# Placing every second head pair on the other partition half in a fused attention and feed-forward kernel

## The chip, the cores and the metric

One Trainium2 chip, one of its cores. The metric is the device time of one execution in microseconds (us), as the median of several runs. The kernel before took 403.56 us (median of 4 runs, 403.14 to 403.96).

The engines are named as the profile names them. PE is the matrix engine, and PEld its weight loads; DVE is the vector engine, ACT the scalar engine with the activation functions, POOL the general engine (GpSimd), SP an engine that here only issues transfers. Each engine works through its own queue in order. PSUM is the memory that PE writes its sums to; DVE and ACT read it and write SBUF, the working memory. Copying a result from PSUM to SBUF is called evicting it. Both memories have 128 partitions, and an engine's cost goes by the elements along a partition.

## What is computed

From the reference, shortened:

```
# q, k, v: (8 batches, 12 heads, 448 positions, 64)
scores = q @ k.T / sqrt(64) - log(448)
attn   = sigmoid(scores) @ v
x      = heads of attn side by side             # 3584 x 768
out    = (silu(x @ w_gate) * (x @ w_val)) @ w_out   # 768 -> 1536 -> 768
```

There is no softmax: each score goes through a sigmoid by itself.

## The kernel before

**Units of attention.** A batch's 12 heads are taken four at a time, which gives 24 units, n = 0 to 23, three to a batch. The four heads of a unit are numbered 2·h2 + w: h2 is the head pair, w the head within the pair. Seven chunks c of 64 key positions make the 448.

**Scores** (`qk_tile`, matmuls at L244). A chunk of a unit is four matmuls of 64 by 64 with 448 columns. The query and key tiles hold pair h2 on partitions 64·h2 onward, so h2 picks the row half of the array; w picks the column half, and with it the PSUM partitions. Bank h2 of a two-bank PSUM tile takes pair h2. One sigmoid on ACT (`sig_tile`, L263; two single-bank ones at L260 at one place in a visit) moves the tile to SBUF as `pt`: head w lies on partitions 64·w onward, for both pairs.

**Attention times values** (`pv`, matmuls at L277). V is loaded with head w on partitions 64·w (`load_v`, L188, one transfer that POOL issues and that turns float32 into float16 on the way). Four matmuls per chunk, one per quadrant of the array. Pair 0 goes to the PSUM half of its own w, pair 1 to the opposite half, since only so all four quadrants are used at once. The next stage wants head w of each pair on partitions 64·w. So pair 0 is evicted by one copy of 128 partitions (L292), and pair 1 by two copies of 64 partitions that cross over (L297 on DVE). Three modes (`how`): 0, all three copies on DVE; 1, one of the crossed copies on ACT after the visit's sigmoids (L305); 2, both on ACT (L300), used once for n = 2.

**Feed-forward, first part.** `ffn1(b, f)` (matmuls at L318) multiplies the six tiles xT[(b, 0..5)] of batch b with one of 12 slices f of w_gate into bank 0 of a PSUM tile and of w_val into bank 1. `ffn1_gate` follows: a sigmoid of bank 0 on ACT (L338), times bank 0 on DVE (L340), times bank 1 on DVE (L344). For f = 0 the order is: tiles 0 to 3 of bank 0, tiles 0 to 3 of bank 1, tiles 4 and 5 of bank 0, tiles 4 and 5 of bank 1, because tiles 4 and 5 come last from attention. For the two last pairs of batches (`LAST - 1` and `LAST`, FAST), eight and twelve slices are instead made by `double`, which does two slices and two batches with seven products (L436) for eight. It needs sums of weights (`fast_w`, DVE, L388), sums of x (`x_sums`, POOL, L409 to L412), evictions by ACT (`snap`, L446) and DVE (L459, L472, L476), and the other activation table (SILU, loaded at L943).

**Feed-forward, second part.** `ffn2_group` (L609) also uses seven products, with sums of h made on DVE (`make_sums`, L530; `budget` says how many after each ffn1) and sums of the remainder on POOL (`rest_sums`, L569). Its evictions go to ACT (L620) for the steps that the string `by` names, else to DVE (L622, L627). The step names are the product numbers 1, 6, 5, 4.

**Order of the work.** PE's order is written out. Up to the ramp's end (about 30 us) it is listed by hand. From there the units of feed-forward work are listed with estimated costs, and "visits" of attention (two to four chunks: two score tiles, then a due `pv`, then the rest of the score tiles, then the sigmoids) are put in between at due times. All PSUM work goes through one ring of four two-bank tiles (`Banked`); a tile can be written again when the readers of its last user are through. A `double` or an ffn1 with f = 0 makes the `pv` that it needs directly ahead of it.

**Transfers.** q and k come through SP (units 4 to 6 through POOL). They are transposed on PE (L214) for the first six units and by transfers that SP issues (L202) from unit 6 on. V and the weights come through POOL's queue. Each transfer that POOL issues takes one of eight semaphores in turn, so POOL may issue a transfer only when the eighth before it has landed.

Of the kernel before, what the change touches and what calls it, by code (L numbers as in the profile page):

```python
# [20 lines left out]
def kernel(  # L21
# [22 lines left out]
    LAST = B // 2 - 1  # L44
# [133 lines left out]
    def load(n, which, eng=None):  # L178
# [4 lines left out]
        (eng or nc.sync).dma_start(out=st, in_=src_of(n, which))  # L183
        qkv_st[(n, which)] = st

    def load_v(n):
        t = v16p.tile([128, 2, S], FP16, tag="v16", name=f"v16_{n}")
        nc.gpsimd.dma_start(out=t, in_=src_of(n, 2))  # L188
        v16[n] = t

    def cast(n, which, eng):
# [43 lines left out]
    xT = {}  # L235

    def qk_tile(n, c, at=None):
        sd = Banked(at=at)
        sc = sd.t
        qt, kt = qT[(n, 0)], qT[(n, 1, c)]  # L240
        for w in range(2):
            for h2 in range(2):
                r = slice(h2 * 64, h2 * 64 + 64)
                nc.tensor.matmul(  # L244
                    out=sc[w * 64:(w + 1) * 64, h2, :S],
                    lhsT=kt[r, w * 64:(w + 1) * 64],
                    rhs=qt[r, :, w * 64:(w + 1) * 64],
                    start=True,
                    stop=True,
                )  # L250
        return sd
# [14 lines left out]
    def pv(n, how=0, at=None):  # L266

        b, j = divmod(n, NJ)
        P = Banked(at=at).t
        vt = v16.pop(n)  # L270
        for c in range(C):
            pt = pts.pop((n, c))
            for h2 in range(2):
                for w in range(2):
                    r = slice(w * 64, w * 64 + 64)
                    g = (w ^ h2) * 64
                    nc.tensor.matmul(  # L277
                        out=P[g:g + 64, h2, :S],
                        lhsT=vt[r, h2, c * D:(c + 1) * D],
                        rhs=pt[r, h2, :],  # L280
                        start=(c == 0),
                        stop=(c == C - 1),
                    )

        def x_tile(h2):
            if n >= NQ - NJ:
                at = 4 * W2 + (2 * j + h2) * S
                return half_of(stg_a)[:, at:at + S]
            return xtp.tile([128, S], FP16, tag="xT", name=f"xT_{b}_{2 * j + h2}")

        x = x_tile(0)
        first = nc.vector.tensor_copy(out=x, in_=P[:, 0, :S])  # L292
        xT[(b, 2 * j)] = x
        x = x_tile(1)
        xT[(b, 2 * j + 1)] = x
        halves = [(x[w * 64:(w + 1) * 64, :], P[(1 - w) * 64:(2 - w) * 64, 1, :S]) for w in range(2)]
        done = [nc.vector.tensor_copy(out=o, in_=i) for o, i in halves[how:]]  # L297
        if how == 2:
            for o, i in halves:
                apart(nc.scalar.copy(out=o, in_=i), first)  # L300

        def rest():
            if how == 1:
                o, i = halves[0]
                apart(nc.scalar.copy(out=o, in_=i), first, *done)  # L305

        return rest


    V, G = nc.vector, nc.gpsimd  # L310
    hT = {}
# [12 lines left out]

    def ffn1(b, f):
        D = Banked("f", made=(b // 2, f))
        for prs in (range(NP - 2), range(NP - 2, NP)) if f == 0 else (range(NP),):
            ffn1_mm(D, b, f, prs)
        ffn1_gate(D, b, f)
        if b % 2:  # L330
            h_sums(b // 2, f)
            make_sums(budget[(b, f)])
        for fn in fill.pop((b, f), ()):
            fn()
# [165 lines left out]
    budget = {}  # L500
# [184 lines left out]
    for pb in range(B // 2):  # L685
# [20 lines left out]
        if pb == 0:  # L706
            fill[(1, 7)] = [lambda: w_sum(0, 3), lambda: w_sum(0, 2)]
            fill[(1, 9)] = [lambda: w_sum(0, 1)]
            o_units += [(0.0, w_sum, a) for a in ((1, 3), (1, 2))]
            part((0, 1, 0, 1), ("1654", "154"), (skip, skip, w((1, 1))))  # L710
            part((0,) * 5, "", (w((0, 4), (1, 4)),))
            copies = [lambda f=f: keep_rest(1, (f, f + 1, f + 2), V.tensor_copy) for f in range(0, NF, 3)]
            part((1,) * 5, "", copies)
            part((2,) * 7, "654")
        elif pb == 1:
            part((0, 1, 0, 1), "1")
            part((0,) * 5)
            part((1,) * 5, "", (lambda: list(rest_sums(1, G)),))
            for g, by in ((2, "54"), (3, "")):
                part((g,) * 3, by)  # L720
                part((g,) * 4, by)
        else:
            part((0, 1) * 7, "1", (skip, lambda: keep_rest(LAST, range(NF), nc.scalar.copy)) if pb < LAST else ())
            if pb == LAST:
                part((3,) * 7)
            part((2,) * 7)
# [22 lines left out]
    def attn_step(group, pvs, how):  # L749
        late = 1 if pvs else 0  # L750
        for part in (group[:2], group[2:]):
            scs = [(n, c, qk_tile(n, c)) for n, c in part]
            rest = [pv(pvs.pop(0), how) for _ in range(len(pvs))]
# [3 lines left out]
            for f in rest:  # L757
                f()

    NPE = 2 * NJ  # L760

# [173 lines left out]
    for i, (fn, args, _) in enumerate(seq):  # L935
        if fn is ffn1:
            ahead = [len(a) if f is None else 0 for f, a, _ in seq[i + 1:i + 3]] + [0, 0]
            budget[args] = 3 if ahead[0] else 0 if ahead[1] == 4 else 2
        if fn is double:
            args[2].append(lambda: make_sums(5))  # L940

# [2 lines left out]
    for fn, args, how in seq:  # L944
        if fn is None:
            pvs, pend = pend, []
            attn_step(args, pvs, how)
# [64 lines left out]
```

## Time and profile before

| | us |
|---|---|
| median of 4 runs | 403.56 |
| the profiled execution, whole time | 403.14 |
| its span (first to last instruction in the profile) | 401.4 |
| outside the span | 1.7 |
| PE busy | 389.2 |
| DVE busy | 262.8 |
| ACT busy | 238.0 |
| POOL busy | 115.1 |
| PE busy from 30 to 397 us | 364.85 of 367 |
| PE busy from 0 to 30 us | 24.35 of 30 |
| mean granted PE clock | 1.00 of full speed |

How to read the rows. A group's row gives line, engine, operation, output and inputs, shape and count, then the busy time and the mean of one in ns, then the engine's idle time ahead of them and what ended it. A row of the timeline gives start, duration, engine, line, operation, count, and in brackets the idle time just before with its releaser. Several instructions of one line are merged into one row, with the count at its end. Ends of matmuls are modelled, so the distance between starts says more about PE than the durations do.

### The profile page before, as it was taken

The page shows a single profiled execution, that of the slowest core. Times are in us where ns is not written, and L with a number is a line of the kernel's source. Part 1 is how long each engine was busy: PE and PEld are TensorE (multiplying, and loading weights), DVE is VectorE, ACT ScalarE, POOL GpSimd, SP SyncE. Part 2 cuts the span into 40 slices and gives each one's busy share as a digit, 9 for nine tenths or more (in the row PEclk, how much of TensorE's full clock was granted, in tenths as well). Part 3 has the DMA queues.
Part 4 walks back from the last instruction along what each step waited for, and adds up shares of the span by engine and source line. Part 5 has one row for each costly group of instructions (what it writes and reads, how often), then busy time and mean ns, then how long its engine had stood idle before and what let it go on. Part 6 is the DMA issues. An engine that isn't in the chain of part 4 may idle for free.

```text
span 401.4 us, 8098 instructions
## 1 busy us (share of the span) xinstructions
PE 389.2 (97%) x3116; PEld 202.4 (50%) x3116; DVE 262.8 (65%) x510; ACT 238.0 (59%) x386; POOL 115.1 (29%) x185
## 2 busy tenths in 40 slices
PE   7799999999999999999999999999999999999995
PEld 3444544445554444444455554444555655555663
DVE  3737657888644555577764457699986568877553
ACT  5965885747457777777753667776654055756000
POOL 4528042311220222222214923910006500000900
PEclk9999999999999999999999999999999999999999
DMA  8999989994599798789785898400000520000055
GB/s 279 243 248 254 246 177 276 167 201 48 136 278 236 161 153 170 162 160 150 174 161 106 227 236 162 47 2 1 2 0 2 157 78 2 2 2 0 2 165 149
DMA packets 65286, 54.39 MB, mean 136 GB/s; under 512 B 35744, under 2 KB 61440, under 8 KB 65248
## 3 DMA queue, kind: packets, MB, share of 16 engines
q1 hardware_dynamic: 49744, 38.22, 37.3%
q0 software_dynamic: 15072, 15.34, 25.0%
q8 instruction: 24, 0.39, 0.5%
q10 hardware_dynamic: 432, 0.33, 0.3%
q14 instruction: 14, 0.11, 0.1%
HBM read 47.19 MB, written 11.01 MB: 145 GB/s over the span
## 4 chain that ended last, share of the span: by engine, by line
PE 91%; DVE 3%; DMA 3%; ACT 1%; issue 1%; SPq 0%; POOL 0%; ACTq 0%; DVEq 0%
PE ps_D L318 32%; PE ps_D L609 24%; PE ps_D L436 20%; PE ps_D L277 8%; PE ps_D L244 8%; DMA v<-in_v_dram 2%; DMA st<-in_q_dram 1%; DVE S L530 1%; DVE xT L297 1%; DVE t L340 0%; PE ps_D L214 0%; ACT pt_a L263 0%; ACT s L338 0%; DVE stg_a L297 0%; DVE xT L292 0%
## 5 line engine op out<-in xcount | busy, mean ns | idle before, releaser
L263 ACT ACTIVATE pt_a<-ps_D 128x896 f16<-128x896 f32 x148 | 127.1, 920 | 42.7 <-PE ps_D L244 41.3
L318 PE MATMUL ps_D<-xT,wg 128*128 128x448 f16 x336 | 74.2, 353 | 0.6 <-DVE t L340 0.5
L318 PE MATMUL ps_D<-xT,wv 128*128 128x448 f16 x336 | 73.7, 352 | 0.0
L340 DVE TENSOR_TENSOR t<-ps_D,s 128x448 f16<-128x448 f32 x56 | 34.9, 624 | 40.4 <-ACT s L338 39.2
L318 PEld LDWEIGHTS <-wg 128*128 128x128 f16 x336 | 30.2, 98 | 36.7 <-issue 12.5
L318 PEld LDWEIGHTS <-wv 128*128 128x128 f16 x336 | 32.8, 98 | 30.8 <-issue 0.4
L446 ACT ACTIVATE snap<-ps_D 128x448 f32<-128x448 f32 x60 | 31.1, 542 | 27.2 <-PE ps_D L436 26.8
L244 PE MATMUL ps_D<-T,T 64*64 64x448 bf16 x644 | 44.4, 357 | 2.7 <-DVE T L220 1.2
L338 ACT ACTIVATE s<-ps_D 128x448 f16<-128x448 f32 x56 | 30.8, 550 | 24.9 <-PE ps_D L318 24.9
L609 PEld LDWEIGHTS <-S 128*128 128x128 f16 x312 | 30.2, 98 | 21.7 <-issue 2.1
L195 POOL CAST c<-stg_a 128x896 bf16<-128x896 f32 x40 | 36.5, 938 | 14.7 <-DMA stg_a<-in_q_dram 10.7
L609 PE MATMUL ps_D<-ramp_a,S 128*128 128x384 f16 x234 | 40.2, 326 | 0.0
L344 DVE SCALAR_TENSOR_TENSOR hT<-ps_D,t 128x448 f16<-128x448 f32 x56 | 35.0, 625 | 5.8
L627 DVE SCALAR_TENSOR_TENSOR osb<-ps_D,osb 128x384 f32<-128x384 f32 x42 | 23.4, 557 | 22.4 <-PE ps_D L609 16.7
L277 PE MATMUL ps_D<-pt_a,v 64*64 64x448 f16 x672 | 36.0, 350 | 0.5 <-DMA v<-in_v_dram 0.5
L622 DVE TENSOR_SCALAR osb<-ps_D 128x384 f32<-128x384 f32 x37 | 20.6, 557 | 18.4 <-PE ps_D L609 15.7
L820 POOL CAST held<-S 128x1 bf16<-128x1 f16 x3 | 0.6, 188 | 107.3 <-ACT osb L620 55.7
L820 POOL CAST held<-pt_a 128x1 bf16<-128x1 f16 x13 | 2.4, 185 | 100.3 <-ACT pt_a L263 100.3
L609 PEld LDWEIGHTS <-hT 128*128 128x128 f16 x228 | 22.0, 98 | 15.8 <-issue 1.3
L292 DVE CAST xT<-ps_D 128x448 f16<-128x448 f32 x21 | 13.1, 624 | 24.0 <-PE ps_D L277 20.9
L244 PEld LDWEIGHTS <-T 64*64 64x64 bf16 x644 | 15.2, 105 | 25.3 <-issue 18.4
L277 PEld LDWEIGHTS <-v 64*64 64x64 f16 x672 | 19.5, 107 | 13.4 <-issue 1.1
(109 smaller groups left out, 503.6 us busy)
## 6 DMA issues: line engine op xcount, KB each, us to landing
out_dram<-osb SPq DMA_DIRECT2D x52, 192.0 KB, 3.2
stg_a<-in_q_dram SPq DMA_DIRECT2D x18, 448.0 KB, 5.7
stg_a<-in_k_dram SPq DMA_DIRECT2D x18, 448.0 KB, 6.4
v<-in_v_dram POOLq DMA_DIRECT2D x24, 224.0 KB, 5.8
wg<-in_moe_w_gate_dram POOLq DMA_DIRECT2D x4, 576.0 KB, 11.9
wv<-in_moe_w_val_dram POOLq DMA_DIRECT2D x4, 576.0 KB, 13.2
wo<-in_moe_w_out_dram POOLq DMA_DIRECT2D x4, 576.0 KB, 8.2
stg_a<-in_q_dram POOLq DMA_DIRECT2D x3, 448.0 KB, 13.8
```

Source lines behind the costliest of these rows:

```text
L195: eng.tensor_copy(out=t.rearrange("p c h d -> p h c d"), in_=st.rearrange("p h (c d) -> p h c d", c=C))
L244: nc.tensor.matmul(out=sc[w * 64:(w + 1) * 64, h2, :S], lhsT=kt[r, w * 64:(w + 1) * 64], rhs=qt[r, :, w * 64:(w + 1) * 64], start=True, st ...
L263: nc.scalar.activation(out=pt, in_=sc[:, :, :S], func=SIGM, bias=sbias, scale=qkscale)
L277: nc.tensor.matmul(out=P[g:g + 64, h2, :S], lhsT=vt[r, h2, c * D:(c + 1) * D], rhs=pt[r, h2, :], start=(c == 0), stop=(c == C - 1),)
L318: nc.tensor.matmul(out=D.t[:, i, :S], lhsT=(wg16, wv16)[i][f // FW][:, pr, cs], rhs=xT[(b, pr)], start=(pr == 0), stop=(pr == NP - 1),),
L338: D.read(nc.scalar.activation(out=s16, in_=D.t[:, 0, :S], func=SIGM), 0)
L340: D.read(nc.vector.tensor_tensor(out=t1, in0=D.t[:, 0, :S], in1=s16, op=MULT), 0)
L344: nc.vector.scalar_tensor_tensor(out=hT[(b // 2, f)][:, b % 2, :], in0=D.t[:, 1, :S], scalar=hsc(b // 2), in1=t1, op0=MULT, op1=MULT),
L436: nc.tensor.matmul(out=D.t[:, bank, :S], lhsT=W(f, j), rhs=X(j), start=(start and j == 0), stop=(stop and j == JT - 1), skip_group_check=True,
L446: D.read(nc.scalar.mul(out=o, in_=D.t[:, bank, :S], mul=scale), bank)
L609: nc.tensor.matmul(out=D.t[:, bank, :hw], lhsT=l, rhs=B_(i), start=(first and i == order[0]), stop=(i == order[-1]), skip_group_check=True,),
L627: D.read(nc.vector.scalar_tensor_tensor(out=o, in0=i, scalar=1.0 / hsc(pb), in1=o, op0=MULT, op1=ADD), bank)
```

## The change

Five edits.

1. For all units but n = 0 (`flip`): the scores of pair 1 go to the opposite PSUM half; V's rows are loaded to match, by two transfers of 64 partitions instead of one of 128 (heads 0 and 3 to the first half, heads 1 and 2 to the second); in `pv` pair 1 uses the opposite row half and its own column half. Both pairs are then evicted by one copy of 128 partitions each: both on DVE, except for n = 2, where the second is on ACT. n = 0 keeps the three copies. The mode that left a copy to ACT behind the sigmoids is gone.
2. ffn1 with f = 0: tiles 0 to 3 of bank 0, 0 to 2 of bank 1, 4 and 5 of bank 0, 3 to 5 of bank 1.
3. In `ffn2_group` for the second pair of batches, group 2: the evictions of steps 5 and 4 go from ACT to DVE.
4. `budget` is 0 for ffn1 (5, 9), so the three sums that were made there are made later.
5. The SILU table is loaded ahead of the `pv` that precedes the first `double`, not behind it.

```
+    def flip(n):
+        return n > 0
+
     def load_v(n):
         t = v16p.tile([128, 2, S], FP16, tag="v16", name=f"v16_{n}")
-        nc.gpsimd.dma_start(out=t, in_=src_of(n, 2))
+        if flip(n):
+            b, j = divmod(n, NJ)
+            src = v[b, 4 * j:4 * j + 4].rearrange("h (p c) d -> p h (c d)", c=C)
+            for w, heads in enumerate((slice(0, 4, 3), slice(1, 3))):
+                nc.gpsimd.dma_start(out=t[w * 64:(w + 1) * 64], in_=src[:, heads])
+        else:
+            nc.gpsimd.dma_start(out=t, in_=src_of(n, 2))
...
                 r = slice(h2 * 64, h2 * 64 + 64)
+                g = (w ^ (h2 and flip(n))) * 64
                 nc.tensor.matmul(
-                    out=sc[w * 64:(w + 1) * 64, h2, :S],
+                    out=sc[g:g + 64, h2, :S],
...
-                    r = slice(w * 64, w * 64 + 64)
-                    g = (w ^ h2) * 64
+                    r, g = w * 64, (w ^ h2) * 64
+                    if flip(n):
+                        r, g = g, r
+                    r = slice(r, r + 64)
...
-        x = x_tile(0)
-        first = nc.vector.tensor_copy(out=x, in_=P[:, 0, :S])
-        xT[(b, 2 * j)] = x
-        x = x_tile(1)
-        xT[(b, 2 * j + 1)] = x
-        halves = [(x[w * 64:(w + 1) * 64, :], P[(1 - w) * 64:(2 - w) * 64, 1, :S]) for w in range(2)]
-        done = [nc.vector.tensor_copy(out=o, in_=i) for o, i in halves[how:]]
-        if how == 2:
-            for o, i in halves:
-                apart(nc.scalar.copy(out=o, in_=i), first)
-        def rest():
-            if how == 1:
-                o, i = halves[0]
-                apart(nc.scalar.copy(out=o, in_=i), first, *done)
-        return rest
+        xs = [x_tile(h2) for h2 in range(2)]
+        first = nc.vector.tensor_copy(out=xs[0], in_=P[:, 0, :S])
+        if not flip(n):
+            for w in range(2):
+                nc.vector.tensor_copy(out=xs[1][w * 64:(w + 1) * 64, :], in_=P[(1 - w) * 64:(2 - w) * 64, 1, :S])
+        elif how == 2:
+            apart(nc.scalar.copy(out=xs[1], in_=P[:, 1, :S]), first)
+        else:
+            nc.vector.tensor_copy(out=xs[1], in_=P[:, 1, :S])
...
     def ffn1(b, f):
         D = Banked("f", made=(b // 2, f))
-        for prs in (range(NP - 2), range(NP - 2, NP)) if f == 0 else (range(NP),):
-            ffn1_mm(D, b, f, prs)
+        if f == 0:
+            for bank, lo, hi in ((0, 0, NP - 2), (1, 0, NP // 2), (0, NP - 2, NP), (1, NP // 2, NP)):
+                ffn1_mm(D, b, f, range(lo, hi), (bank,))
+        else:
+            ffn1_mm(D, b, f, range(NP))
...
-            for g, by in ((2, "54"), (3, "")):
-                part((g,) * 3, by)
-                part((g,) * 4, by)
+            for g in (2, 3):
+                part((g,) * 3)
+                part((g,) * 4)
...
-            budget[args] = 3 if ahead[0] else 0 if ahead[1] == 4 else 2
+            budget[args] = 0 if args == (2 * LAST - 1, 9) else 3 if ahead[0] else 0 if ahead[1] == 4 else 2
...
+        if fn is double and silu:
+            silu.pop()()
         if pend and (fn is ffn1 and args[1] == 0 and (args[0], NP - 1) not in xT or fn is double or how):
             for n in pend:
-                pv(n, 1 if how else 0)()
+                pv(n)
             pend = []
-        if fn is double and silu:
-            silu.pop()()
```

`attn_step` loses its argument `how` and calls `pv` in the same place as before.

More of the change, by code (lines that the diff above doesn't have):

```diff
@@ L289, in x_tile @@
             return xtp.tile([128, S], FP16, tag="xT", name=f"xT_{b}_{2 * j + h2}")
-        x = x_tile(0)
-        first = nc.vector.tensor_copy(out=x, in_=P[:, 0, :S])
-        xT[(b, 2 * j)] = x
-        x = x_tile(1)
-        xT[(b, 2 * j + 1)] = x
-        halves = [(x[w * 64:(w + 1) * 64, :], P[(1 - w) * 64:(2 - w) * 64, 1, :S]) for w in range(2)]
-        done = [nc.vector.tensor_copy(out=o, in_=i) for o, i in halves[how:]]
-        if how == 2:
-            for o, i in halves:
-                apart(nc.scalar.copy(out=o, in_=i), first)
-        def rest():
-            if how == 1:
-                o, i = halves[0]
-                apart(nc.scalar.copy(out=o, in_=i), first, *done)
-        return rest
+        xs = [x_tile(h2) for h2 in range(2)]
[7 more added lines that the diff above has]
+            nc.vector.tensor_copy(out=xs[1], in_=P[:, 1, :S])
+        for h2 in range(2):
+            xT[(b, 2 * j + h2)] = xs[h2]
     V, G = nc.vector, nc.gpsimd
@@ L747, with attn_step @@
             vtime.append(t0 + (at - n0) / (n1 - n0) * (t1 - t0))
-    def attn_step(group, pvs, how):
+    def attn_step(group, pvs):
         late = 1 if pvs else 0
@@ L752, in attn_step @@
             scs = [(n, c, qk_tile(n, c)) for n, c in part]
-            rest = [pv(pvs.pop(0), how) for _ in range(len(pvs))]
+            while pvs:
+                pv(pvs.pop(0))
             for i, (n, c, sc) in enumerate(scs):
                 sig_tile(n, c, sc, split=len(group) == 4 and part[0] == group[0] and i == late)
-            for f in rest:
-                f()
     NPE = 2 * NJ
@@ L946 @@
             pvs, pend = pend, []
-            attn_step(args, pvs, how)
+            attn_step(args, pvs)
             for n, c in args:
```

## The prediction

> **What bounds the kernel now.** I read the page's busy line, then the granted clock, the chain that ended last, and then the timeline wherever two starts of PE lay further apart than the work between them.
>
> ```profile
> span 401.4 us, 8098 instructions
> PE 389.2 (97%) x3116; PEld 202.4 (50%) x3116; DVE 262.8 (65%) x510; ACT 238.0 (59%) x386; POOL 115.1 (29%) x185
> PEclk9999999999999999999999999999999999999999
> PE 91%; DVE 3%; DMA 3%; ACT 1%; issue 1%; SPq 0%; POOL 0%; ACTq 0%; DVEq 0%
> L297 DVE CAST xT<-ps_D 64x448 f16<-64x448 f32 x36 | 22.4, 621 | 0.8
> L292 DVE CAST xT<-ps_D 128x448 f16<-128x448 f32 x21 | 13.1, 624 | 24.0 <-PE ps_D L277 20.9 <-ACT pt_a L263 2.6
> ```
>
> PE is the bound: 97% busy at the full clock, 91% of the chain. So DVE or ACT work that goes away is worth nothing by itself; it is worth what PE waits for it. The last two rows show what the change removes: a copy of 64 partitions takes 621 ns, one of 128 takes 624. Two crossed copies cost double.
>
> PE's starts give its pitch. Six matmuls of L318 last 1.30 us with 0.35 for one, so (1.30 - 0.35)/5 = 0.19 us each. A change between 64x64 and 128x128 matmuls adds 0.09. Against that pitch, four places between 30 and 397 us are late for a reason that the change touches (first column start, second duration):
>
> ```profile
> 126.13 0.54 ACT L338 ACTIVATE s<-ps_D 128x448 f16<-128x448 f32 x1 [0.41 <-PE ps_D L318]
> 126.40 0.76 PE L244 MATMUL ps_D<-T,T 64*64 64x448 bf16 x12
> 126.71 0.62 DVE L340 TENSOR_TENSOR t<-ps_D,s 128x448 f16<-128x448 f32 x1 [1.02 <-ACT s L338]
> 127.38 1.30 PE L318 MATMUL ps_D<-xT,wg 128*128 128x448 f16 x6 [0.22 <-DVE t L340]
> ...
> 224.92 2.12 PE L609 MATMUL ps_D<-ramp_a,S 128*128 128x384 f16 x12
> 227.07 0.51 ACT L620 ACTIVATE osb<-ps_D 128x384 f32<-128x384 f32 x1
> 227.63 1.14 PE L609 MATMUL ps_D<-wo,S 128*128 128x384 f16 x6 [0.59 <-ACT osb L620]
> ...
> 235.60 2.12 PE L609 MATMUL ps_D<-ramp_a,S 128*128 128x384 f16 x12
> 237.56 1.14 PE L609 MATMUL ps_D<-wo,S 128*128 128x384 f16 x6
> ...
> 263.37 1.26 DVE L297 CAST stg_a<-ps_D 64x448 f16<-64x448 f32 x2
> 264.68 0.76 PE L244 MATMUL ps_D<-T,T 64*64 64x448 bf16 x12 [0.58 <-DVE stg_a L297]
> ...
> 271.15 0.98 ACT L446 ACTIVATE snap<-ps_D 128x448 f32<-128x448 f32 x2
> 271.84 1.29 PE L436 MATMUL ps_D<-xS,stg_a 128*128 128x448 f16 x6 [0.20 <-ACT snap L446]
> 272.12 1.16 DVE L459 TENSOR_TENSOR small<-ps_D,snap 128x448 f32<-128x448 f32 x2
> 272.97 1.30 PE L436 MATMUL ps_D<-xS,wv 128*128 128x448 f16 x6
> ```
>
> The reader is to see four waits, each with its releaser above it. The pair at 224.92 and 235.60 matters most: the same piece of code, 2.71 us to the next group with step 5 evicted on ACT, 1.96 with it on DVE.
>
> **The change part by part.** The sum is against the profiled execution, 403.14 us (span 401.4 plus 1.7).
>
> *Reorder in ffn1, f = 0 (edit 2).* At 127.38 PE wants the tile of f = 0 back and waits for bank 0's last matmul, then the sigmoid, then L340. From 126.40, twelve score matmuls and the switch take 0.69 (as from 264.68 to 265.37), so it is 0.98 - 0.69 = 0.29 late. The next f = 0 does the same: 166.35 to 167.40, 0.36 late. Bank 0 now ends one matmul earlier: 0.19 at each. The earlier matmuls need xT 4 and 5 one pitch sooner, and the second comes 0.62 sooner with one copy less. **0.38**. The f = 0 at 63.4 has no visit behind it and no wait: nothing.
>
> *Steps 5 and 4 to DVE (edit 3).* ACT does three sigmoids from 224.66 to 227.2 and only then L620, which frees the bank. DVE is idle there for 2.72 us. The twin at 235.60 shows the step on DVE with no wait: 2.71 - 1.96 = **0.75**. The trace puts DVE's idle time down to an output transfer, but the stores of that buffer (issued 214.3) took about 3 us. Step 4 moves from ACT at 229.78 to DVE, idle then until 231.65: nothing.
>
> *Sums moved, fewer copies, table earlier (edits 4, 5, 1).* From 251.73 two banks of ffn1 take 2.38 us to the next visit; from 261.65 to 264.68 it is 3.03, so 0.65 late. DVE did three sums (0.35 each) ahead of the three copies. Without them and with two copies, DVE is done at 261.40 + 1.26 = 262.7, well before 264.0. At 271.84 PE is 0.37 late (twelve matmuls from 269.20 should take 2.27): ACT loaded the table (1.28) behind its half copy. Together 1.02, if nothing else is late next. Something is: at 272.97 PE needs L459 done. DVE now starts L340 for (5, 10) at 263.83 instead of 264.66, but must fit the three sums (1.0 with their dependences) before the two `fast_w`, so it reaches the L340 of (5, 11) at 267.7 against 268.11. The work from there to L459 is the same: 272.12 - 0.4, first half done 272.3, against 272.97 now. **0.6** of the 1.02.
>
> *Copies elsewhere.* DVE loses 17 copies (41 half copies become 24), 10.6 us; ACT loses 6, 3.2 us. Where PE does not wait for them: nothing. In the ramp PE waits at 21.61 for the last copy of unit 1; 0.62 sooner frees it 0.2 sooner, but w_val's first part lands at 9.78 + 12.7 = 22.5 and is used at 22.78. **0.05**.
>
> *Quadrants.* The four score matmuls still use four quadrants; in `pv` the third and fourth swap. 28 matmuls take 1.49 now: (1.49 - 0.35)/6 = 0.19 per four, so all four run together although pairs share a row half. Scores, in another order, also have 0.19. I take nothing; a loss is a rival below.
>
> [...]
>
> *V in two transfers (edit 1).* 23 more issues on POOL at about 0.73: 16.8 us on an engine with 286 idle. Behind them in POOL's queue in the ramp stand weights and casts, and one more of the eight semaphores is used up each time, so w_gate's third part, issued at 26.83 now, would wait for unit 4's q (13.01 + 17.6 = 30.6). The casts of unit 5 move behind it, from 35.9 to about 37.3, and end near 39.1; PE transposes them at 40.4. The queue itself is the limit there: V's take 0.9 to 1.2 us from landing to landing, weights 2.9, without gaps until 52. So what counts is the added time per split, d. The tight use is w_val's third part, behind four splits: issued 32.77, landed 9.0 later at 41.8, used here:
>
> ```profile
> 42.33 0.92 PE L318 MATMUL ps_D<-xT,wv 128*128 128x448 f16 x4
> wv<-in_moe_w_val_dram POOLq DMA_DIRECT2D x1, 576.0 KB, 9.0
> ```
>
> With 0.2 for the weight load and semaphore, 0.3 us of slack. Bounds for d: 0, as half the bytes take half the time (below that nothing speaks for a gain); above, a half that takes as long as a whole, 1.0. The spread of whole V's, 0.3, lies between. I take 0.05, from the row that is nearest: the output stores are transfers of 64 partitions too, and four of them pass in about 2 us. Then 4d = 0.2: hidden. Later V's land 11 us or more ahead of use. The tightest later work behind a V on POOL is the casts of unit 21 (228.0): 0.73 later, their second transpose lands near 236.7 instead of 235.97, and PE wants it at 239.6 less the gains, 238.4.
>
> [...]
>
> **Sum:** 0.38 + 0.75 + 0.6 + 0.05 = 1.78. 403.14 - 1.78 = 401.36 for the profiled execution; the median stands 0.42 above it, so 401.8.
>
> **Rivals.**
> 1. *The waits move.* DVE gets later than I worked out in the first `double`, or ACT's sigmoids still stand ahead of the freed tile at 127 and 167. For: L459 already takes 0.4 of the gain. Against: the twin's 0.75 needs no such care. Then about 0.75: 402.8.
> 2. *The V halves delay w_val.* Place: the matmul at 42.33. It decides from 4d = 1.78 + 0.3, d = 0.52. At d = 1.0: 4.0 - 0.3 - 1.78 = 1.9 slower, 405.5. For: an engine's fixed time per transfer isn't in the trace by itself. Against: the stores.
> 3. *The quadrants don't overlap in the new order.* Pairs in turn would add 0.19 to each of 161 chunks: 30 us, 432. For: no row has this order. Against: two other orders both have 0.19.
>
> **How the numbers follow.** Forecast 0.64: 401.8, own range 401.1 to 402.5 (ramp 0.2 more and DVE 0.4 more; or one small term missing). Rival 1 0.19, around the border of what counts as faster: 0.07 faster, 0.12 same. Rival 2 0.13: 0.04 same, 0.09 slower. Rival 3 0.04, slower. A difference of 0.2% (0.8 us) is about what a measurement of this kernel can tell from no change. Faster 0.71, same 0.16, slower 0.13. The range reaches into rivals 1 and 2: 401.0 to 404.0.
>
> **What would show it.** In the profile after: about 1.96 between the two L609 groups near 224; no DVE releaser ahead of the visit near 263; PE's visit near 126 about 0.1 late; L459's successor as the next wait near 271; w_val's third part landing before 42; 28 `pv` matmuls still 1.49 us. I am wrong if PE waits for a transfer near 42, or if `pv` takes longer.

## The result, and the profile after

The changed kernel takes 402.4 us (median of 35 runs, 401.05 to 404.51) against 403.57 before (55 runs, 403.14 to 405.13). The ratio is 0.9971, with a 95% interval from 0.9963 to 0.9978: 1.2 us faster, where 1.8 was forecast. The runs also lie further apart: the median stands 1.35 above the lowest, before 0.43. The profiled execution took 402.61, its span is 400.5; against the profiled one before (403.14, the lowest of its runs) that is only 0.53 less. First the page of the changed kernel (share of the chain by engine; groups with busy time, mean ns of one, idle time before them):

```profile
span 400.5 us, 8096 instructions
PE 388.7 (97%) x3116; PEld 201.9 (50%) x3116; DVE 247.3 (62%) x495; ACT 234.1 (58%) x378; POOL 125.8 (31%) x208
PE 87%; DMA 9%; POOL 1%; ACT 0%; DVE 0%; issue 0%; SPq 0%; DVEq 0%; ACTq 0%
L323 PE MATMUL ps_D<-xT,wv 128*128 128x448 f16 x336 | 73.7, 352 | 1.0 <-DMA wv<-in_moe_w_val_dram 1.0
L195 POOL DMA_DIRECT2D v<-in_v_dram x46 | 27.5, 601 | 11.7 <-DMA wv<-in_moe_w_val_dram 4.6
```

DVE has lost 15 us, and that shows nowhere by itself: PE is still 97% busy. What is new is the share of DMA in the chain, 9% where it was 3%, and PE's 1.0 us of waiting for w_val. Its place is the one that rival 2 names. The timeline of PE there (first column start, second duration; in brackets PE's idle time and what ended it):

```profile
41.43 1.30 PE L323 MATMUL ps_D<-xT,wg 128*128 128x448 f16 x6
43.78 1.31 PE L323 MATMUL ps_D<-xT,wv 128*128 128x448 f16 x6 [1.05 <-DMA wv<-in_moe_w_val_dram]
45.01 0.57 PE L254 MATMUL ps_D<-T,T 64*64 64x448 bf16 x8
45.42 1.49 PE L289 MATMUL ps_D<-pt_a,v 64*64 64x448 f16 x28
```

The six matmuls of w_val should start 1.14 after those of w_gate and start 2.35 after them: 1.21 lost. The last line answers rival 3: 28 `pv` matmuls still take 1.49, so its 30 us are not there. Now PE at the four places of the prediction (same columns):

```profile
127.86 0.76 PE L254 MATMUL ps_D<-T,T 64*64 64x448 bf16 x12
128.65 1.29 PE L323 MATMUL ps_D<-xT,wg 128*128 128x448 f16 x6
...
225.90 2.12 PE L617 MATMUL ps_D<-ramp_a,S 128*128 128x384 f16 x12
227.86 1.14 PE L617 MATMUL ps_D<-wo,S 128*128 128x384 f16 x6
...
263.03 1.30 PE L323 MATMUL ps_D<-xT,wv 128*128 128x448 f16 x6
264.25 0.76 PE L254 MATMUL ps_D<-T,T 64*64 64x448 bf16 x12
...
268.77 2.44 PE L444 MATMUL ps_D<-xT,wg 128*128 128x448 f16 x12
271.06 1.30 PE L444 MATMUL ps_D<-xS,stg_a 128*128 128x448 f16 x6
```

From the visit to the next group: 0.79, so 0.10 late instead of 0.29. Between the two L617 groups: 1.96, the twin's figure. Ahead of the visit near 264 and of the group near 271 no wait is left at all.

Where the time went is best summed from PE's starts: the time from start to start, less the matmul's own work, in each stretch (us):

```
            0-60   60-100  100-220  220-260  260-300  300-400
before     12.46    1.90     7.69     3.11     2.29     1.39
after      13.90    1.90     7.21     2.40     1.22     1.36
```

Behind 60 us the change gains 2.29; in the first 60 it loses 1.44 in this execution. Of these, 0.23 are there at 22 us already: V of unit 0 landed at 13.23 instead of 12.81, and the q and k ahead of it were late too. (That made 0.42; the shorter copies of unit 1 gave 0.20 of it back near 21.8.) Unit 0 is not touched by the change, so I put that down to chance. The other 1.21 is the wait above.

Two sets of numbers say how w_val gets late. Landings of the software queue, from the trace's semaphore events (last engine done, us; V's in halves show the second half):

```
          v2     wg1    wv1    q4     k4     v3     q5     k5     v4     wg2    wv2
before   23.67  26.54  29.41  30.60  31.77  32.76  33.91  35.07  36.08  38.96  41.81
after    23.29  26.13  29.35  30.94  32.80  33.90  35.34  37.08  37.99  40.86  43.73
```

Up to w_val's second part (wv1) the halves cost nothing: V of unit 2 takes 1.13 behind the weights ahead of it, 1.22 before. From there to w_val's third part (wv2) the queue loses 2.0 (14.38 against 12.40), and it loses it at q and k: 1.59, 1.86, 1.44 and 1.74 from landing to landing, where before each took 1.15 to 1.19. V of unit 4 takes 0.91, less than before. The packets say the same. Those of 5376 bytes, which only q and k of units 4 to 6 have, took 208 ns on average between 30 and 34 us before, and 304 after; of all 480, one took over 300 ns before, 127 after. The packets of V (896 bytes, 88 ns before 45 us) and of the weights (768, 79 ns) are unchanged. So the halves are not slow; the wide transfers beside them are. Nor is it w_val's own issue, 33.81 instead of 32.77: the transfer ahead of it was then still in the queue (wg2, landed at 40.86).

The wait is not in every execution. Two kernels of the experiments below have the same halves in the same places up to here: the change with POOL busy for longer, and the layout alone. PE at this place, first in the one, then in the other:

```profile
41.52 1.30 PE L323 MATMUL ps_D<-xT,wg 128*128 128x448 f16 x6
42.66 1.31 PE L323 MATMUL ps_D<-xT,wv 128*128 128x448 f16 x6
...
41.55 1.30 PE L323 MATMUL ps_D<-xT,wg 128*128 128x448 f16 x6
42.72 1.31 PE L323 MATMUL ps_D<-xT,wv 128*128 128x448 f16 x6
```

There w_val's third part landed at 42.62 and 42.67, just in time: 1.14 and 1.17 from start to start, so 0.03 of wait at most. The packets were slow in both (269 and 265 ns). So slow packets come with the halves each time; the wait of 1.21 is seen in one execution of three.

### The profile page after: what moved, and what is told of

The parts are those of the page before. It is cut to its first block, busy times and chain, and to the rows that moved or that the text cites. A ratio compares the mean times of both kernels' runs of the same rounds, so it can differ in the third digit from the quotient of the medians.

```text
span 400.5 us, 8096 instructions
## 1 busy us (share of the span) xinstructions
PE 388.7 (97%) x3116; PEld 201.9 (50%) x3116; DVE 247.3 (62%) x495; ACT 234.1 (58%) x378; POOL 125.8 (31%) x208
## 4 chain that ended last, share of the span: by engine, by line
PE 87%; DMA 9%; POOL 1%; ACT 0%; DVE 0%; issue 0%; SPq 0%; DVEq 0%; ACTq 0%
PE ps_D L323 29%; PE ps_D L617 24%; PE ps_D L444 20%; PE ps_D L254 7%; PE ps_D L289 7%; DMA stg_a<-in_q_dram 4%; DMA wv<-in_moe_w_val_dram 2%; DMA v<-in_v_dram 2%; DMA ramp_a<-in_q_dram 1%; POOL c L204 1%; SPq L166 0%; ACT osb L628 0%; POOL wg L138 0%; DVE t L348 0%; DVE osb L630 0%
## 5 line engine op out<-in xcount | busy, mean ns | idle before, releaser
L348 DVE TENSOR_TENSOR t<-ps_D,s 128x448 f16<-128x448 f32 x56 | 34.9, 624 | 53.7 <-ACT s L346 52.6
L617 PEld LDWEIGHTS <-S 128*128 128x128 f16 x312 | 30.2, 98 | 20.9 <-issue 1.3
L617 PE MATMUL ps_D<-ramp_a,S 128*128 128x384 f16 x234 | 40.2, 326 | 0.0
L630 DVE TENSOR_SCALAR osb<-ps_D 128x384 f32<-128x384 f32 x39 | 21.7, 557 | 20.3 <-PE ps_D L617 17.4
L195 POOL DMA_DIRECT2D v<-in_v_dram x46 | 27.5, 601 | 11.7 <-DMA wv<-in_moe_w_val_dram 4.6
L617 PEld LDWEIGHTS <-hT 128*128 128x128 f16 x228 | 22.1, 98 | 15.6 <-issue 1.3
```

What stands on the lines that cost most here:

```text
L195: nc.gpsimd.dma_start(out=t[w * 64:(w + 1) * 64], in_=src[:, heads])
L348: D.read(nc.vector.tensor_tensor(out=t1, in0=D.t[:, 0, :S], in1=s16, op=MULT), 0)
L617: nc.tensor.matmul(out=D.t[:, bank, :hw], lhsT=l, rhs=B_(i), start=(first and i == order[0]), stop=(i == order[-1]), skip_group_check=True,),
```

## The experiments

The theory after this reading had three parts. (1) V's in halves of 64 neighbouring partitions slow the wide transfers beside them (304 ns for a packet of 5376 bytes, before 208), w_val's third part comes late, and this eats a part of the gain that differs from run to run. (2) The gain itself comes from the four small edits; the layout that names the change gives nothing, since PE waited for the copies at one or two places only, and there for another reason too: (3) the sums on DVE ahead of the visit near 264 were three times as long as elsewhere (1.05 and 1.07 against 0.35), because POOL was adding at the same time. The rivals: chance (that execution's slow packets), the number of transfers instead of their form, and the copies.

All numbers first. "Span" is the median span of the runs, "outside" the mean of time less span, "packet" the mean of the 5376-byte packets between 30 and 34 us of the profiled execution, "w_val" the landing of its third part there.

| kernel | time, us | ratio to before (95%) | span | outside | packet, ns | w_val, us |
|---|---|---|---|---|---|---|
| before | 403.45 to 403.57 | | 401.7 | 1.78 | 208 | 41.81 |
| the change | 402.40 | 0.9971 (0.9963 to 0.9978) | 400.3 | 2.08 | 304 | 43.73 |
| early V's whole | 401.35 | 0.9951 (0.9937 to 0.9965) | 399.6 | 1.80 | 208 | 41.57 |
| before, V in halves | 405.15 | 1.0044 (1.0030 to 1.0058) | 402.9 | 2.26 | 248 | 41.83 |
| before, V by half rows | 404.30 | 1.0019 (1.0010 to 1.0029) | 402.0 | 2.31 | 208 | 41.73 |
| before, V even and odd | 404.51 | 1.0024 (1.0015 to 1.0034) | 402.2 | 2.30 | 207 | 41.97 |
| V of 4 behind w_val | 401.79 | 0.9953 (0.9940 to 0.9967) | 399.6 | 2.22 | 316 | 43.13 |
| V of 3 and 4 behind w_val | 403.51 | 1.0005 (0.9985 to 1.0026) | 401.25 | 2.23 | 226 | 39.90 |
| change without layout | 404.86 | 1.0026 (1.0016 to 1.0036) | 402.8 | 2.00 | 209 | 42.70 |
| only the sums | 402.90 | 0.9979 (0.9970 to 0.9988) | 401.1 | 1.80 | 207 | 42.15 |
| change, POOL longer | 403.46 | 0.9993 (0.9982 to 1.0005) | 401.7 | 1.78 | 269 | 42.62 |
| all but the layout | 402.01 | 0.9963 (0.9949 to 0.9977) | 399.85 | 2.13 | 208 | 41.75 |
| only the layout | 403.88 | 0.9998 (0.9984 to 1.0012) | 401.95 | 1.97 | 265 | 42.67 |
| only the steps | 403.04 | 0.9982 (0.9971 to 0.9993) | 400.9 | 2.14 | 209 | 41.61 |

The column "outside" was not expected to do anything; it is constant within 0.1 for each kernel and differs by 0.5 between kernels. So spans are compared too, below.

One more number from the landings. From w_val's second part to its third the queue takes 12.38 to 12.42 in seven kernels without halves of neighbouring partitions there. It takes 13.13, 13.43, 13.55 and 14.38 in the four that have those of units 3 and 4 in between (before with V in halves, only the layout, the change with POOL longer, the change). One kernel with whole V's stands out: the change without the layout, 13.45, of which 1.04 came at unit 4's q, with packets of 209 ns. Why is not known.

### Early V's whole

```diff
     def flip(n):
-        return n > 0
+        return n > 5
```

Units 1 to 5 keep the crossed copies as well (unit 2's two on ACT, as before).

> The changed kernel with the new layout only from unit 6 on: units 1 to 5, whose V stands in the queue with the early weights, keep one whole V transfer and the three copies. Theory (the halves of the early V's make w_val's third part late; the rest of the change is worth about 2.1): w_val's third part lands near 41.8 and is not waited for, the packets of 5376 bytes of units 4 and 5 (q and k) take about 207 ns as before, and the time is 1.9 to 2.2 below before, about 401.4. Rival (that execution's slow packets were chance and the early halves cost nothing): as the change, 1.2 below before, with its scatter of 1.3 between the lowest and the median run.

401.35, 2.1 below before, and four of five runs within 0.3 of the lowest. The packets take 208 ns, w_val lands at 41.57 and PE does not wait for it. The theory's numbers, and chance is out as a full explanation: the same 18 later units in the new layout, the same four edits, and the wait is gone with the early halves. This is the fastest kernel of the study; its interval touches that of the change. By the median spans (399.6 and 400.3) the early halves cost 0.7.

### Before, with V in halves

```diff
-        nc.gpsimd.dma_start(out=t, in_=src_of(n, 2))
+        for w in range(2):
+            nc.gpsimd.dma_start(out=t[w * 64:(w + 1) * 64], in_=src_of(n, 2)[w * 64:(w + 1) * 64])
```

(from unit 1 on; the same in the next two.)

> Before, with one edit: every V from unit 1 on is loaded in two transfers of 64 partitions each, to the same places. Theory (halves make w_val late): PE waits about 1 us at the second half of f = 0's neighbour near 42, and the time is 0.8 to 1.3 above before, about 404.6. Rival (chance, or the copies and the scores' new order are to blame): within 0.3 of before. My forecast's own price for a split (0.05 each, 0.3 of slack) gives 0.

Slower by 1.7, more than the theory said. The packets are slow (248 ns), but in the profiled execution, the fastest of nine, w_val lands at 41.83 and PE does not wait there; the median stands 1.0 above it. That w_val's wait makes this 1.0 is likely and not shown. What the profile does show is a cost that nobody had named, 0.44 at the visit near 264. Timelines of PE and DVE in this kernel:

```profile
265.16 0.76 PE L248 MATMUL ps_D<-T,T 64*64 64x448 bf16 x12 [1.02 <-DVE stg_a L301]
...
260.42 0.65 DVE L534 TENSOR_TENSOR S<-hT,hT 128x384 f16<-128x384 f16 x1
261.11 1.07 DVE L534 TENSOR_TENSOR S<-S,hT 128x384 f16<-128x384 f16 x1
262.10 1.18 DVE L534 TENSOR_TENSOR S<-hT 128x384 f16<-128x384 f16 x1
```

PE's wait is 1.02 where it was 0.58. The three sums ahead of the copies take 2.90 together, 2.47 before: POOL, behind its second V transfers, makes its sums of x 0.6 to 0.8 later, so the third sum falls beside one of them as well. This gave part (3) of the theory.

### Before, with V by half rows, and with even and odd partitions

```diff
+            nc.gpsimd.dma_start(out=t[:, w], in_=src_of(n, 2)[:, w])
```
```diff
+            nc.gpsimd.dma_start(out=t[w::2], in_=src_of(n, 2)[w::2])
```

> Before, with one edit: every V from unit 1 on is loaded in two transfers of 128 partitions, one for each half of a partition's row, so the same number of transfers, bytes and semaphores as with two halves of 64 partitions. If the number of transfers costs (issues on POOL, semaphores, a fixed time), the loss is that of the two halves, 0.8 to 1.3. If it is the narrow form (64 partitions at a time), none: within 0.2 of before.

> Before, with one edit: every V from unit 1 on in two transfers of 64 partitions, but of the even and of the odd partitions instead of the lower and the upper half. Two halves made the packets of 5376 bytes of units 4 and 5 take 248 to 316 ns between 30 and 34 us, two transfers of all 128 partitions left them at 208. [...] Rival (64 partitions at a time are too few, wherever they lie): 250 ns or more, 405.0 or more.

Each splits V in two transfers of the same bytes. In both the packets stay at 207 or 208 ns, with 64 partitions at a time in the second: so neither the count nor the 64 is to blame, but that the 64 are neighbours. The rival (too few partitions wherever they lie) falls. Why neighbouring ones slow the wide packets is not shown; the records have the packets' times alone.

By the times alone my expectation for the half rows would have pointed the wrong way: 0.85 slower, the number that I had given to the count of transfers. But PE does not wait for w_val in it. The span is 0.3 longer than before and the time outside the span 0.53; the wait near 264 is 0.38 longer, for POOL's reason above. The three kernels share these two costs (2.26 to 2.31 outside, 0.38 to 0.48 near 264), so the price of the halves of neighbouring partitions is what is left: 0.7 to 0.9 by the median spans (402.9 against 402.2 and 402.0). An expectation in total time doesn't tell a cause apart when the edit has a second effect.

### V of unit 4, and of units 3 and 4, behind w_val's third part

```diff
-    load_v(4)
     w_load("g", 2)
...
     w_load("v", 2)
+    load_v(4)
     load_v(5)
```

> The changed kernel with unit 4's V loaded behind w_val's third part instead of ahead of w_gate's. It has 3.5 us more before it is late. Theory (what stands ahead of w_val in the queue is what costs): w_val's third part lands at least the 0.9 of that V earlier, and the wait of 1.2 near 43.8 falls to 0.3 or less: 0.8 to 1.0 below the change, 401.5. Rival (slow packets that come with the change wherever the V stands, or chance): 0.3 below the change at most, 402.1 or more.

401.79: a gain of 0.6 on the change, between the theory and the rival, with 401.2 as the lowest run. The packets are still slow (316 ns: unit 3's halves stand where they were), and w_val lands at 43.13. In its profiled execution PE came later than that for another reason, told at the end. Moving unit 3's V as well (its line behind `load(4, 1, G)` goes too):

> The changed kernel with the V's of units 3 and 4 behind w_val's third part. No half stands between the q and k of units 4 and 5 then; unit 3's V has about 1.5 us before it is late. Theory (a half beside wide transfers slows their packets): the 5376-byte packets before 40 us take about 208 ns again, w_val's third part lands before 41 and is never waited for, and the time is 1.2 to 1.5 below the change's, 400.9 to 401.3, with little scatter. Rival (the halves slow the queue wherever they stand, or unit 3's V is waited for now): 401.8 or more.

Here the theory was half right. The packets are nearly normal (226 ns) and w_val lands at 39.90, 3.8 earlier than in the change. The time is no better than before all the same, and the scatter is large (402.72 to 406.94). PE:

```profile
42.01 0.56 PE L223 MATMUL ps_D<-idn,c 128*128 128x128 bf16 x7 [1.38 <-POOL c L204]
42.88 0.56 PE L223 MATMUL ps_D<-idn,c 128*128 128x128 bf16 x7 [0.30 <-POOL c L204]
```

PE waits for POOL's casts of unit 5. Six halves of V are now issued in a row behind w_val (33.63 to 37.1, 0.6 each), and the casts stand behind them. I had weighed where unit 3's V would land, not what its issue stands ahead of. This is one execution; what made the slowest runs is not known.

### The change without the layout (every crossed copy on DVE)

```diff
     def flip(n):
-        return n > 0
+        return False
```

> The changed kernel without its first part: no head pair changes its half, every V is one transfer, every unit has its crossed copies (three, on DVE; unit 2's two on ACT, as before). Left are the order in the first tile, the evictions moved to DVE, the sums moved and the table load moved. Theory (these make the gain; the new layout itself gives nothing, since PE never waited for the copies except near 264): 1.7 to 2.1 below before, 401.4 to 401.8, with w_val's third part landing near 41.8. Rival (the layout is needed for the gain near 264 and 271, 1.0 of it): 1.1 or less below before, 402.4.

Wrong: 1.3 slower than before. The kernel does not isolate what I meant. Before, five units, those evicted beside the second part of the block or at the end of a stage, had one crossed half on ACT (`how` = 1); the changed code has no such path, and without the layout the third copy lands on DVE there. PE's waits of this kernel near 208 and 227:

```profile
208.45 3.08 PE L620 MATMUL ps_D<-wo,hT 128*128 128x384 f16 x18 [0.54 <-DVE xT L310]
...
226.93 1.14 PE L620 MATMUL ps_D<-ramp_a,S 128*128 128x384 f16 x6 [0.24 <-DVE osb L633]
```

So DVE has no room for a third copy in that stage: by PE's starts 0.71, 0.41 and 0.41 near 208, 227 and 237, 0.58 near 114, 0.84 near 277. What the miss shows is a thing the layout does buy: all copies on DVE without ACT.

### All but the layout, with the copies as before

Before, with the order in the first tile, the steps, the sums and the table load, and no other edit.

> Before, with the other edits alone: the order in the first tile (0.38), steps 5 and 4 to DVE (0.75), the three sums moved (0.63 by the run with this edit alone) and the table load ahead of the last copies (the 0.36 near 271). Scores, V's, and the crossed copies with their halves on ACT stay as before. Theory (these four make the gain, the layout none): 1.8 to 2.1 below before, 401.4 to 401.7. Rival (the layout with its whole copies is needed, as the run without it that put every crossed copy on DVE was slower than before): 1.2 or less below before.

402.01, 1.5 below before, 1.9 in the median span. That is short of the theory's 1.8 to 2.1 and better than the rival's 1.2. Seven of the twelve runs lie between 401.64 and 402.07, five between 402.89 and 403.22. The profiled one is of the upper group, and has this wait of PE, with DVE's line for it:

```profile
72.67 1.29 PE L318 MATMUL ps_D<-xT,wg 128*128 128x448 f16 x6 [1.01 <-DVE t L343]
...
70.77 1.32 DVE L533 TENSOR_TENSOR S<-S,hT 128x384 f16<-128x384 f16 x1
```

POOL's issues of W_out and its casts of unit 7 (69.39 to 72.9) fell on two sums (1.12 and 1.32) that stand ahead of a tile of ffn1 which PE wanted back; before, they fell on the next two in DVE's order (1.45 and 1.08), for which nobody waited. That such a fall makes the upper group is a guess from one profile. The four other runs of that group have the lowest granted clocks of the twelve (0.991 to 0.996), so the clock is another candidate, and neither is shown.

### Only the layout

The changed kernel with the four other edits taken back.

> Before, with the first part alone: scores and V of every unit but the first in the new halves, V in two transfers, two whole copies, none on ACT but unit 2's. The order in the first tile, steps 5 and 4 on ACT, the three sums and the table load's place stay as before. Theory (halves make w_val late by 1.2 on the median; against it the copies save 0.6 at the wait near 264 and the half copy's 0.36 near 271, while POOL, later by the second transfers, slows a sum by 0.4): 0.3 to 0.9 above before, 403.9 to 404.5. Rival (the layout pays by itself): 0.3 or more below before.

0.9998, from 0.9984 to 1.0012: no change that can be measured. By the medians it is 0.37 above before, at the lower edge of the theory's range. The rival (pays by itself, 0.3 or more) finds no support in that, but the interval reaches to 0.65 below before and does not exclude it. The packets are slow again (265 ns). The wait near 264 is 0.31 instead of 0.58 and the one near 271 is gone, so PE does gain from the copies there; that the halves lose about as much is argued from the total, since in this execution PE did not wait for w_val.

### Only the sums

```diff
-            budget[args] = 3 if ahead[0] else 0 if ahead[1] == 4 else 2
+            budget[args] = 0 if args == (2 * LAST - 1, 9) else 3 if ahead[0] else 0 if ahead[1] == 4 else 2
```

> Before, with one edit: the three sums on DVE ahead of the last visit but one are not made there but later. Before they took 1.05, 1.07 and 0.35 us there, 2.5 together, while POOL added too; elsewhere they take 0.35 each. Theory (the wait near 264 was these sums, not the number of copies): the wait of 0.65 is gone with three copies still there; where the sums go POOL is idle and they take 0.35 each; 0.4 to 0.65 below before. Rival (the copies made it): no more than 0.2 below before.

402.90, 0.63 below the 403.53 beside it: with three copies still there, the wait near 264 is gone. These are the lines of DVE and POOL before:

```profile
260.38 1.05 DVE L530 TENSOR_TENSOR S<-hT,hT 128x384 f16<-128x384 f16 x1
261.46 1.07 DVE L530 TENSOR_TENSOR S<-S,hT 128x384 f16<-128x384 f16 x1
262.46 0.35 DVE L530 TENSOR_TENSOR S<-hT 128x384 f16<-128x384 f16 x1
...
260.18 1.04 POOL L411 TENSOR_TENSOR xS<-xT,xT 128x448 f16<-128x448 f16 x1
261.17 1.15 POOL L412 TENSOR_TENSOR xS<-xT,xS 128x448 f16<-128x448 f16 x1
```

and these the sums in the changed kernel, where POOL is done at 263.1:

```profile
265.32 0.35 DVE L538 TENSOR_TENSOR S<-hT,hT 128x384 f16<-128x384 f16 x1
265.71 0.36 DVE L538 TENSOR_TENSOR S<-S,hT 128x384 f16<-128x384 f16 x1
265.98 0.35 DVE L538 TENSOR_TENSOR S<-hT 128x384 f16<-128x384 f16 x1
```

Before, each of the two sums beside an operation of POOL ends 0.21 after it (261.43 and 261.22; 262.53 and 262.32); the one behind POOL's last takes 0.35.

### The change with POOL busy for longer

```diff
-            for f in x_sums(pb, j):
+            fs = x_sums(pb, j)
+            for f in fs * (2 if j == NJ - 1 else 1):
                 f()
```

> The changed kernel with POOL's last four sums of x made twice (the same values), so that POOL adds until about 267.2 instead of 263.1, over the place where DVE makes its three sums now (265.3 to 266.3, 0.35 each). Theory (a sum on DVE with two fp16 inputs from SBUF waits while POOL runs such an operation): the sums there take about 1 us each until POOL is done, DVE gets 1 to 1.5 late, and PE waits near 271 for the sum with the snapshot: 0.6 to 1.2 above the change. Rival (the sums were slow for their own inputs, or behind something else): 0.35 each, and the time of the change within 0.2.

(The same line serves the last pair of batches near 304 to 319 us too, where the third sum is made in place: there the repeated sums have other values, and the last pair's output with them. PE loses nothing there.) DVE, POOL and PE of this kernel:

```profile
264.21 1.05 DVE L538 TENSOR_TENSOR S<-hT,hT 128x384 f16<-128x384 f16 x1
265.30 1.07 DVE L538 TENSOR_TENSOR S<-S,hT 128x384 f16<-128x384 f16 x1
266.30 0.35 DVE L538 TENSOR_TENSOR S<-hT 128x384 f16<-128x384 f16 x1
...
264.02 1.03 POOL L419 TENSOR_TENSOR xS<-xT,xT 128x448 f16<-128x448 f16 x1
265.01 1.15 POOL L420 TENSOR_TENSOR xS<-xT,xS 128x448 f16<-128x448 f16 x1
...
270.62 1.31 PE L444 MATMUL ps_D<-xS,stg_a 128*128 128x448 f16 x6 [0.52 <-DVE stg_a L396]
272.22 1.29 PE L444 MATMUL ps_D<-xS,wv 128*128 128x448 f16 x6 [0.28 <-DVE small L467]
```

The very sums that took 0.35 in the change take 1.05 and 1.07 with POOL adding beside them, again 0.21 past POOL's end, and the third, behind POOL's last, 0.35. PE loses 1.37 between 260 and 280 by its starts, 1.06 by the medians and 1.4 by the median spans (402.40 and 400.3 for the change, in another set of runs). That settles part (3): it is POOL, not the sums' inputs. What holds a sum until POOL is through is not shown; the trace has the 0.21 us from the end of the one to the end of the other.

### Only the steps

```diff
-            for g, by in ((2, "54"), (3, "")):
-                part((g,) * 3, by)
-                part((g,) * 4, by)
+            for g in (2, 3):
+                part((g,) * 3)
+                part((g,) * 4)
```

> Before, with one edit: steps 5 and 4 of that group evicted on DVE and not on ACT. Theory: 0.75 below before, the wait near 227.6 gone, nothing else moved: 402.7 to 402.9. Rival (the wait was for a transfer of the output, and moves with the step): 0.2 below before at most.

The wait near 227 is gone and no other is new; the median span is 0.8 shorter. The time is only 0.47 lower, since 2.14 lie outside the span where before 1.78 do. By the trace the theory holds; by the time alone it would be 0.3 short.

## Why the prediction was right, and where not

The direction and the range held, with the size 0.6 too good. That is the remainder of three errors, one of them in the change's favour, so the hit is partly luck: 402.4 lies 0.1 inside the range, and without the 0.5 that the error of item 3 gave it would lie outside.

1. *The order in the first tile.* 0.29 late became 0.10 near 127; near 168 the distance from the start of the last score matmul to the next group went from 0.63 to 0.44. 0.38 in all, as worked out.
2. *Steps 5 and 4.* 0.75 of wait gone, 1.96 between the groups. As worked out; the twin was the right row.
3. *Sums, copies, table.* Two readings failed. "DVE did three sums (0.35 each)" was the price of the common row; in that place they took 2.47, readable in the timeline of before, and they were the wait near 264 by themselves. That did not move the term, since the 0.65 came from PE's starts. What moved it is "the work from there to L459 is the same". DVE came to L348 of (5, 11) at 267.71, as worked out, but from there to the addition with the snapshot (L467, 271.24) it took 3.53, where before it took 4.01 (268.11 to 272.12). Of the 0.48, the two copies give 0.22: they start 0.53 apart, before 0.63 and 0.65. The rest came at the sums ahead of them, which were other ones. So the 0.4 of "what is late next" never came, and the term was 1.07 instead of 0.6. That the three sums fell behind POOL's end in their new place was not worked out; beside POOL's additions they would have cost 1.4, as the run with POOL busy for longer shows.
4. *V in two transfers.* The step that failed is "d = 0.05, so 4d = 0.2: hidden". The price of the split's own transfers was right, even less than that: V of units 2, 3 and 4 took 1.13, 1.10 and 0.91 where whole ones took 1.22, 0.99 and 1.01. The slack was even larger than the 0.3: 0.2 had been taken off for weight load and semaphore, and PE started 0.05 after the landing (43.73 and 43.78). The cost fell on their neighbours in the queue, which the sum had at no price: q and k of units 4 and 5, 1.9 later in the profiled execution. Spread on the four splits that is 0.48 each, just at the 0.52 from which rival 2 was to decide. Rival 2 had the right place and the wrong owner of the price. The prediction's own sign of being wrong, a wait of PE for a transfer near 42, is there in the profiled execution. By the medians (2.20 of gains less 1.47 of span) the first 60 us cost 0.7, which fits the 0.7 of the early halves and the 0.7 to 0.9 of the halves added to before. That this is w_val's wait in the runs without a trace is likely and not shown.
5. *Outside the span.* "Span 401.4 plus 1.7" was taken as fixed. It is 1.78 before and 2.08 after: 0.30 that no row shows.
6. *Quadrants, copies elsewhere.* The quadrants cost nothing (28 `pv` matmuls take 1.49 in both), as worked out. For the 0.05 of the copies in the ramp, PE's step at 21.6 does come 0.20 sooner behind the matmuls ahead of it (0.32 instead of 0.52); whether w_val's first part would then hold it is not shown, as V of unit 0 was late in this execution.

Together 0.38 + 0.75 + 1.07 - 0.73 - 0.30 = 1.17, the measured difference; the 0.73 is what is left over when the rest is known, not a measurement of its own.

What stays open: how often w_val is waited for in the change's other runs (their scatter of 1.3 against 0.4 fits a wait that comes and goes, and so do the two other traces of this ramp, which are without it); and what the time outside the span consists of. Most of the scatter is not the clock: the change's runs with a granted clock of 0.999 or 1.00, 19 of 36 with the profiled one, lie between 401.05 and 403.91, those of before, 45 of the 87 beside the experiments, between 403.07 and 404.17. The order in the first tile and the place of the table load were not run alone; their share is read from traces. Near 271 the wait also goes away with the layout alone, and without the layout when the other four edits are made, so either is enough there.

## What to carry to other kernels

Price a transfer that is split by what it does to the transfers beside it, not only by its own landing: where halves of neighbouring partitions stood among wide ones, the wide ones' packets took a fifth to a half longer (248 to 316 ns against 208); two transfers over all partitions did not do that (207 and 208). Read a duration at its own place: an operation that takes 0.35 in most rows took 1.05 beside another engine's additions; moving it away ended the wait near 264, where fewer copies alone left 0.31 of 0.58. And do one part alone with everything else as it was: the kernel that I took for "all but the layout" had lost ACT's share of the copies as well.

## What the runs showed of the hardware that was not expected

- In six profiles with V in two halves of neighbouring partitions ahead of w_val, the 5376-byte packets took 226 to 316 ns; in eight with whole V's there, or two transfers over all partitions, 207 to 209. The lowest of the six, 226, is the kernel that has no half between unit 4's q and w_val.
- PE's wait near the start had two prices. Where V of unit 0 came so late that PE stood for 1.10 us, the granted clock was 0.83 of full speed in that stretch, and 28 matmuls took 2.83 instead of 1.52. Timeline of PE, and the stretch from 10 to 20 us (the third figure from the right is the granted clock), of the kernel with V of unit 4 behind w_val:

```profile
13.64 2.83 PE L289 MATMUL ps_D<-pt_a,v 64*64 64x448 f16 x28 [1.10 <-DMA v<-in_v_dram]
...
10.00:20.00 10.00, 7.08 (x91) 3.50 (x93) 5.95 (x11) 7.89 (x11) 7.00 (x9) 0.83 1.22 258
```

  The change without the layout did the same after 1.15; after 0.31 to 0.92 of waiting, in the twelve other profiles, the clock stayed at 1.00. Unit 0 has one whole V in every kernel here, so this is no part of the change, but it cost these two executions 1.3 us each at that place.
- The time outside the span is a trait of each kernel, within 0.1 of its mean in all its runs: 1.78 to 1.80 for four of them, 1.97 to 2.31 for the others. It follows neither the number of V transfers (the change with POOL longer has as many as the change, and 1.78) nor any one edit.
